# Chunk 0 loaded as three transfers of 1 MB, its attention run tensor by tensor

## The chip, the cores and the metric

The kernel runs on one core of a Trainium2 chip. The metric is the device time of one execution in microseconds (us); lower is better.

The core has a TensorE (PE in the profile, with its weight loads as PEld), a VectorE (DVE), a ScalarE (ACT), a GpSimd (POOL) and a SyncE (SP). Each has its own stream of instructions and runs it in order. The streams wait for each other through semaphores. Transfers between HBM and on-chip memory are issued from the streams of SP, ACT and POOL, and appear in the profile as the queues q1 (issued on SP), q10 (ACT) and q0 (POOL).

## The reference

The input is q, k and v of shape (4 batches, 8 heads, 768 steps, 64) in float32 and two weights. A linear attention with a decay per head feeds a two-layer network with GELU:

```
for t in 0..767:
    state = gamma_h * state + outer(k_t, v_t)        # per batch and head, 64 x 64
    y_t   = scale * q_t @ state
x   = y as (3072 tokens, 512)
out = gelu_tanh(x @ w_in) @ w_out                    # 512 -> 2048 -> 512
```

## The kernel before

**Tiling.** The 768 steps are cut into six chunks of 128 (`C`). For a chunk `c` and a batch `b` the attention has these steps, each a helper:

- `prep1(eng, nm, c, b)` casts one of q, k, v of one batch (128 steps x 8 heads x 64) to float16 on the engine named, with the decay multiplied in (line 162) or as a plain copy (`copy_on`, lines 149 and 151).
- `mm_T` (line 192) transposes q and k of a batch on TensorE, eight instructions, and `ev_T` copies them to on-chip memory as `qkT`.
- `mm_A` (line 217) makes the 128 x 128 products of k and q within a chunk, and `ev_A` (line 230) multiplies them by `mask` on VectorE into `a_sb`, two buffers per half.
- `mm_yc` (line 241) adds the part of the earlier state and does nothing for chunk 0. `mm_yi` (line 254) makes the part within the chunk, and `ev_Y` copies the result to `xT`.
- `mm_s` (line 278) makes this chunk's addition to the state, and `ev_S` folds it into `st`. The state is first needed by Y of chunk 1.

The first layer of the network is called M1 here: `moe1` (512 tokens, one block of 128 features) and `moe1_two` (two blocks of features, a range of tokens `t0` to `t1`), both through `moe1_mm` (line 363), with a GELU on ScalarE (line 379). `t01` is the tokens of batches 0 and 1, `t2` and `t3` those of batches 2 and 3. The second layer of chunk 0 is `moe2` (line 397). For chunks 1 to 5 the two layers are made from sums of quarter blocks (lines 434, 507 and 622), which take most of the span.

**Order.** There is no planner. The kernel is written under a manual schedule: each engine runs its instructions in the order in which the Python calls stand. Chunk 0 is written out by hand, and the change lies there. `spin(n)` puts n matmuls of zeros on TensorE (line 126).

**Loads.** `load1(eng, nm, c, b)` (line 89) moves one tensor of one batch and chunk, 256 KB. `load(nm, c, eng)` (line 95) moves a tensor of all four batches, 1 MB, on SP unless told otherwise; it is used from chunk 2 on. Chunk 0 comes as twelve `load1`, dealt out over SP and ACT in the order in which the batches need them:

```
    nc.sync.dma_start(out=cst[:, :OT + 128], in_=cst_h.ap())
    load1(nc.scalar, "q", 0, 0)
    load1(nc.sync, "k", 0, 0)
    load1(nc.scalar, "v", 0, 0)
    ...
```

`cst` holds the decays and the triangle from which VectorE makes `mask` (line 137, eight instructions), and `iden` is the identity for the transposes. `load_w_in(i)` (line 344) and `load_w_out(i)` (line 353) each move one quarter of a weight from float32 to float16, 1 MB read and 512 KB written, on POOL. POOL reaches `load_w_in(0)` behind its scaling of k of batch 1, and the other three behind that of batch 2. `hold` (line 102) is a one-element copy on POOL that keeps chunk 1's loads back until a weight has landed.

**Chunk 0.** The batches go one after the other: prep, transposes, A, Y and S of batch 0, then of batch 1, and so on, with spins between them. Y of batches 0 and 1 stands before M1, and batches 2 and 3 are woven into M1's first groups. M1's groups 4 and 5 are made as two ranges of 256 tokens, groups 6 to 15 with all 512.

Of the kernel before, what the change touches and what calls it, by code (L numbers as in the profile page):

```python
# [9 lines left out]
F16 = mybir.dt.float16  # L10
# [6 lines left out]
def kernel(  # L17
# [9 lines left out]
    nc = tc.nc  # L27
    B, H, S, Dh = q.shape
# [59 lines left out]
    def load1(eng, nm, c, b):  # L88
        eng.dma_start(
            out=ld_tile(nm, c, b),  # L90
            in_=srcs[nm][b, :, c * C:(c + 1) * C, :].rearrange("h p d -> p h d"),
        )
# [8 lines left out]

        nc.gpsimd.tensor_copy(out=ld_tile(nm, c, b)[0:1, 0, 0:1], in_=until)

    nc.sync.dma_start(out=cst[:, :OT + 128], in_=cst_h.ap())
    load1(nc.scalar, "q", 0, 0)
    load1(nc.sync, "k", 0, 0)
    load1(nc.scalar, "v", 0, 0)
    nc.sync.dma_start(out=iden, in_=iden_h.ap())
    load1(nc.sync, "q", 0, 1)
    load1(nc.scalar, "k", 0, 1)  # L110
    load1(nc.sync, "v", 0, 1)
    load1(nc.sync, "k", 0, 2)
    load1(nc.sync, "q", 0, 3)
    load1(nc.sync, "v", 0, 3)


    zero = const.tile([128, 512], F16, name="zero")
# [5 lines left out]
    def spin(n):  # L123
        ps = bank("h", shape=(128, 512), name="spin_ps")
        for _ in range(n):
            nc.tensor.matmul(
                out=ps, lhsT=zero[:, 0:128], rhs=zero, start=True, stop=True
            )
# [16 lines left out]
    h16 = {}  # L145
# [7 lines left out]
    def prep1(eng, nm, c, b):  # L153
        t = pre.tile(
            [128, H, Dh], F16, tag=f"{nm}16", bufs=B, name=f"{nm}16"
        )
        src = ld_tile(nm, c, b)
        if (nm == "v") == (c < 2):
            copy_on(eng, t, src)
        else:  # L160
            col = OQ if nm == "q" else OK
            eng.tensor_tensor(  # L162
                out=t,
                in0=src,
                in1=cst[:, col:col + H].unsqueeze(2).broadcast_to([128, H, Dh]),
                op=ALU.mult,
            )
        h16[nm, c, b] = t

    def pair(t, hp):  # L170
        return t[:, 2 * hp:2 * hp + 2]
# [16 lines left out]
    def mm_T(c, b):  # L188
        ps = bank("att", F16, (128, 2, NHP, 128), "qkT_ps")
        for i, nm in enumerate("qk"):  # L190
            for hp in range(NHP):
                nc.tensor.transpose(  # L192
                    out=ps[:, i, hp], in_=pair(h16[nm, c, b], hp), identity=iden
                )
        pss["T", c, b] = ps
# [6 lines left out]
    def ev_T(c, b, eng=nc.vector):  # L202
        copy_on(eng, qkT_of(c, b), pss.pop(("T", c, b)))

    def dma_T(nm, c, *bs):
        for b in bs:
            nc.sync.dma_start_transpose(
                out=qkT_of(c, b)[:, "qk".index(nm)],
                in_=h16[nm, c, b].rearrange("p h d -> p (h d)"),
            )  # L210

    def mm_A(c, b):
        t = qkT[c, b]
        ps = [bank("att", name=f"a_ps{j}") for j in range(2)]
        for hp in range(NHP):
            for j in range(2):
                nc.tensor.matmul(  # L217
                    out=ps[j][:, hp],
                    lhsT=t[j * 64:(j + 1) * 64, 1, hp],
                    rhs=t[j * 64:(j + 1) * 64, 0, hp],  # L220
                    start=True,
                    stop=True,
                )
        pss["A", c, b] = ps

    def ev_A(c, b):
        ps = pss.pop(("A", c, b))
        for j in range(2):
            s = att.tile([128, NHP, 128], F16, tag=f"a{j}", bufs=2, name=f"a_sb{j}")
            nc.vector.tensor_tensor(out=s, in0=ps[j], in1=mask[:, j], op=ALU.mult)  # L230
            a_sb[c, b, j] = s

    def mm_yc(c, b, tag):
        y_ps = pss["Y", c, b] = bank(tag, name="y_ps")
        if c == 0:
            return

        for hp in range(NHP):
            for j in range(2):
                sl = slice(j * 64, (j + 1) * 64)  # L240
                nc.tensor.matmul(  # L241
                    out=y_ps[sl, hp],
                    lhsT=st[sl, b, hp],
                    rhs=qkT[c, b][sl, 0, hp],
                    start=(hp == 0),
                    stop=False,
                    skip_group_check=True,
                )

    def mm_yi(c, b):  # L250
        y_ps = pss["Y", c, b]
        for hp in range(NHP):
            for j in range(2):
                nc.tensor.matmul(  # L254
                    out=y_ps[j * 64:(j + 1) * 64, hp],
                    lhsT=h16["v", c, b][:, 2 * hp + j],
                    rhs=a_sb[c, b, j][:, hp],
                    start=(c == 0),
                    stop=True,
                    skip_group_check=True,  # L260
                )

    def ev_Y(c, b, eng=nc.vector):
        if c not in xT:
            xT[c] = xp.tile([128, NHP, B * C], F16, tag="x", bufs=2, name="xT")
        x, ps = xT[c][:, :, b * C:(b + 1) * C], pss.pop(("Y", c, b))
        if c < 2:
            copy_on(eng, x, ps)
        else:
            nc.vector.tensor_tensor(out=x, in0=ps, in1=dec, op=ALU.mult)  # L270

    def mm_s(c, bs, tag="att"):
        if c + 1 >= NCk:
            return
        s_ps = pss["S", c, bs] = bank(tag, shape=(128, len(bs), NHP, 64), name="s_ps")
        for i, b in enumerate(bs):
            for h in range(H):
                nc.tensor.matmul(  # L278
                    out=s_ps[h % 2 * 64:(h % 2 + 1) * 64, i, h // 2],
                    lhsT=h16["k", c, b][:, h],  # L280
                    rhs=h16["v", c, b][:, h],
                    start=True,
                    stop=True,
                )

    def ev_S(c, bs, eng=nc.vector):
        if c + 1 >= NCk:
            return
        s_ps = pss.pop(("S", c, bs))
        t = st[:, bs[0]:bs[-1] + 1]  # L290
        if c == 0:
            copy_on(eng, t, s_ps)
            return
        for hp in range(NHP):
            nc.vector.scalar_tensor_tensor(
                out=t[:, :, hp],
                in0=t[:, :, hp],
                scalar=cst[:, OG + hp:OG + hp + 1],
                in1=s_ps[:, :, hp],
                op0=ALU.mult,  # L300
                op1=ALU.add,
            )
# [40 lines left out]
    def load_w_in(i):  # L343
        nc.gpsimd.dma_start(
            out=w_in_sb[i],
            in_=moe_w_in.rearrange("(kc p) n -> p kc n", p=128)[
                :, :, w_in_at[i] * 128:(w_in_at[i] + w_in_n[i]) * 128
            ],
        )
# [36 lines left out]
    def moe1_two(c, fp, t0, t1):  # L386

        h_ps = bank("h", shape=(128, 2, B * C // 2), name="h_ps")
        for r in range(2):
            moe1_mm(c, 2 * fp + r, h_ps[:, r, 0:t1 - t0], t0, t1)  # L390
        gelu(g_tile(c, 2 * fp)[:, :, t0:t1], h_ps[:, :, 0:t1 - t0])
# [269 lines left out]
    half = 2 * C  # L661


    load1(AC, "q", 0, 2)
    load1(AC, "v", 0, 2)
    spin(14)
    prep1(VE, "q", 0, 0)
    prep1(PO, "k", 0, 0)
    prep1(AC, "v", 0, 0)
    mm_T(0, 0)  # L670
    ev_T(0, 0, AC)
    load1(AC, "k", 0, 3)
    prep1(VE, "q", 0, 1)
    prep1(PO, "k", 0, 1)
    spin(3)
    mm_A(0, 0)
    ev_A(0, 0)
    mm_T(0, 1)
    ev_T(0, 1, AC)
    prep1(AC, "v", 0, 1)  # L680
    spin(2)
    mm_yc(0, 0, "o")
    mm_yi(0, 0)
    mm_s(0, (0,), "o")
    ev_Y(0, 0, AC)
    prep1(VE, "q", 0, 2)

    load_w_in(0)
    prep1(PO, "k", 0, 2)
    for i in range(1, 4):  # L690
        load_w_in(i)
    prep1(PO, "k", 0, 3)
    prep1(PO, "q", 0, 3)
    for i in range(NO):
        load_w_out(i)
    mm_A(0, 1)
    ev_A(0, 1)
    spin(3)
    mm_T(0, 2)
    ev_T(0, 2, AC)  # L700
    spin(2)
    mm_yc(0, 1, "o")
    mm_yi(0, 1)
    mm_s(0, (1,), "o")
    ev_Y(0, 1, AC)
    prep1(AC, "v", 0, 2)
    spin(2)
    mm_A(0, 2)
    ev_A(0, 2)
    ev_S(0, (0,), AC)  # L710
    prep1(AC, "v", 0, 3)
    ev_S(0, (1,), AC)
    spin(6)
    mm_T(0, 3)
    ev_T(0, 3)


    t01, t2, t3 = (0, half), (half, half + C), (half + C, 2 * half)
    moe1_two(0, 0, *t01)
    mm_A(0, 3)  # L720
    ev_A(0, 3)
    mm_yc(0, 2, "o")
    mm_yi(0, 2)
    mm_s(0, (2,))
    ev_Y(0, 2, AC)
    moe1_two(0, 1, *t01)
    ev_S(0, (2,))
    moe1_two(0, 0, *t2)
    moe1_two(0, 1, *t2)
    mm_yc(0, 3, "o")  # L730
    mm_yi(0, 3)
    mm_s(0, (3,))
    ev_Y(0, 3)
    ev_S(0, (3,))
    moe1_two(0, 2, *t01)
    for fp in range(2):
        moe1_two(0, fp, *t3)
    moe1_two(0, 2, half, 2 * half)

    hold("q", 1, 0, w_out_sb[2][0:1, 0, 0:1])  # L740
    for fc in range(6, NF):
# [210 lines left out]
```

## Time and profile before

| | us |
|---|---|
| median of 3 runs (lowest to highest) | 207.66 (206.92 to 209.23) |
| the profiled execution, its own time | 207.1 |
| its span, first to last instruction | 205.0 |
| PE busy | 195.2 (95%) |
| DVE, ACT, POOL busy | 128.3, 120.6, 110.8 |
| start of M1 of chunk 0 | 18.45 |
| start of the second layer of chunk 0 | 34.81 |

The span is counted from the first to the last instruction of one execution; its own time has 2.1 us more around it. The busy share of an engine is a mean over stages with different limits. The chain of waits, followed back from the last instruction, is 82% TensorE's own work and 8% waiting for transfers. In a line of the timeline the columns are start, length, engine, line of the kernel, operation, output and input, and the count. Lines that read `q1 hardware_dynamic: a, b, c%` give the packets, the megabytes and the share of the sixteen DMA engines of one queue in a stretch of time. The list of DMA issues gives the KB of one transfer and the microseconds from issue to landing; for the transfers of 1 MB the size in this list is misread as 0.2 KB.

### The profile page before, as it was taken

To read this page: it belongs to the slowest core of one execution; us is meant where nothing else is said; L and a number is where in the kernel's file an instruction comes from. 1 tells how busy PE (TensorE), PEld (TensorE's weight loads), DVE (VectorE), ACT (ScalarE), POOL (GpSimd) and SP (SyncE) were. 2 spreads that over 40 slices of the span, in tenths; PEclk is the share of its full clock that TensorE was granted. 3 is DMA by queue.
4 is the path that set the end of the run, shared out by engine and by line. 5 is a ranking of instruction groups with operands and counts; after the bars stand their busy time and mean duration, and the time that the engine had idled before them with its cause. 6 is when DMAs were issued, how large, how long until landed. Compare 5 with 4: busy or idle time off the path is not lost.

```text
span 205.0 us, 5216 instructions
## 1 busy us (share of the span) xinstructions
PE 195.2 (95%) x2120; PEld 151.6 (74%) x2120; DVE 128.3 (63%) x259; ACT 120.6 (59%) x229; POOL 110.8 (54%) x112
## 2 busy tenths in 40 slices
PE   7868999999999989999999999999999999999993
PEld 2445744445778867788887888888888888888882
DVE  3335796429876689989853888836697723445421
ACT  2481566143478457853978585878555587675411
POOL 0597001223103993926399948399955797599000
PEclk9999999999999999999999999999999999999999
DMA  7999999989899993459958869953100220002204
GB/s 160 288 261 206 206 207 221 287 203 297 238 328 220 240 313 84 100 118 298 253 135 202 229 146 307 95 156 128 26 3 0 101 107 0 5 0 106 102 26 179
DMA packets 60759, 33.73 MB, mean 165 GB/s; under 512 B 40960, under 2 KB 57728, under 8 KB 60736
## 3 DMA queue, kind: packets, MB, share of 16 engines
q1 hardware_dynamic: 42624, 22.66, 43.9%
q0 software_dynamic: 4304, 4.46, 12.7%
q10 hardware_dynamic: 13808, 6.29, 11.9%
q8 instruction: 16, 0.26, 0.5%
q14 instruction: 7, 0.06, 0.1%
HBM read 27.63 MB, written 6.29 MB: 165 GB/s over the span
## 4 chain that ended last, share of the span: by engine, by line
PE 82%; DMA 8%; DVE 3%; ACT 3%; issue 1%; ACTq 1%; POOL 0%; DVEq 0%
PE o_ps L507 28%; PE h_ps L622 23%; PE h_ps L363 13%; PE o_ps L397 7%; DMA w_in<-in_moe_w_in_dram 5%; PE y_ps L254 3%; PE a_ps L217 3%; DMA k<-in_k_dram 3%; PE y_ps L241 3%; ACT g L379 1%; DVE xT L270 1%; PE qkT_ps L192 1%; PE s_ps L278 1%; ACTq L95 1%; DVE t_x L434 1%
## 5 line engine op out<-in xcount | busy, mean ns | idle before, releaser
L434 POOL TENSOR_TENSOR s_g<-g 128x512 f16<-128x512 f16 x34 | 38.7, 1151 | 11.6 <-ACT g L379 11.6
L379 ACT ACTIVATE g<-h_ps 128x512 f16<-128x512 f32 (+1 forms) x50 | 28.8, 581 | 22.9 <-PE h_ps L363 17.7
L230 DVE TENSOR_TENSOR a_sb<-a_ps,mask 128x512 f16<-128x512 f32 x48 | 30.2, 684 | 8.8 <-PE a_ps L217 8.4
L507 PE MATMUL o_ps<-t_w,s_g 128*128 128x256 f16 x240 | 34.2, 273 | 0.0
L507 PEld LDWEIGHTS <-s_g 128*128 128x128 f16 x320 | 31.3, 98 | 3.6
L363 PE MATMUL h_ps<-xT,w_in 128*128 128x256 f16 (+2 forms) x232 | 30.4, 284 | 1.2 <-DMA w_in<-in_moe_w_in_dram 0.7
L622 PE MATMUL h_ps<-t_x,s_w 128*128 128x256 f16 x192 | 28.9, 273 | 0.3 <-DVE h_p L434 0.3
L622 PEld LDWEIGHTS <-s_w 128*128 128x128 f16 x256 | 24.4, 98 | 4.7 <-issue 1.2
L363 PEld LDWEIGHTS <-w_in 128*128 128x128 f16 x232 | 20.6, 98 | 8.5 <-issue 0.9
L507 PEld LDWEIGHTS <-g 128*128 128x128 f16 x240 | 23.4, 98 | 2.8
L507 PE MATMUL o_ps<-w_out,g 128*128 128x256 f16 x160 | 22.9, 273 | 0.0
L162 POOL TENSOR_TENSOR v<-v,cst 128x512 f16<-128x512 f32 x16 | 16.2, 1038 | 11.2 <-DMA v<-in_v_dram 11.2
L434 POOL TENSOR_TENSOR s_g<-s_g,g 128x512 f16<-128x512 f16 x17 | 19.6, 1155 | 4.6 <-PE o_ps L507 3.4
L639 ACT COPY h_u<-h_ps 128x512 f32<-128x512 f32 x16 | 9.4, 586 | 21.3 <-PE h_ps L622 21.3
L434 DVE TENSOR_TENSOR h_q<-h_ps,h_q 128x512 f32<-128x512 f32 x16 | 11.1, 692 | 16.3 <-PE h_ps L622 10.4
L622 PEld LDWEIGHTS <-w_in 128*128 128x128 f16 x192 | 18.3, 98 | 3.4 <-issue 0.7
L434 POOL TENSOR_TENSOR s_g<-g,s_g 128x512 f16<-128x512 f16 x17 | 19.5, 1156 | 0.5
L434 DVE TENSOR_TENSOR h_p<-h_ps,h_p 128x512 f32<-128x512 f32 x16 | 11.0, 690 | 13.7 <-ACT h_p L639 9.4
L622 PE MATMUL h_ps<-xT,w_in 128*128 128x256 f16 x128 | 19.2, 272 | 0.3 <-ACT g L379 0.3
L162 POOL TENSOR_TENSOR k<-k,cst 128x512 f16<-128x512 f32 x8 | 8.8, 1094 | 17.7 <-DMA k<-in_k_dram 16.3
L434 DVE TENSOR_TENSOR o_sb<-o_ps,o_sb 128x512 f32<-128x512 f32 (+1 forms) x18 | 10.8, 597 | 7.6 <-PE o_ps L507 7.3
L397 PE MATMUL o_ps<-w_out,g 128*128 128x512 f16 x64 | 14.8, 379 | 0.0
(71 smaller groups left out, 301.0 us busy)
## 6 DMA issues: line engine op xcount, KB each, us to landing
out_dram<-o_sb SPq DMA_DIRECT2D x8, 512.0 KB, 2.7
w_in<-in_moe_w_in_dram POOLq DMA_DIRECT2D x4, 512.0 KB, 9.9
w_out<-in_moe_w_out_dram POOLq DMA_DIRECT2D x4, 512.0 KB, 14.6
k<-in_k_dram SPq DMA_DIRECT2D x6, 256.0 KB, 4.9
v<-in_v_dram ACTq DMA_DIRECT2D x6, 256.0 KB, 5.6
q<-in_q_dram SPq DMA_DIRECT2D x6, 256.0 KB, 5.2
out_dram<-o_sb SPq DMA_DIRECT2D x4, 256.0 KB, 4.4
q<-in_q_dram ACTq DMA_DIRECT2D x2, 256.0 KB, 4.9
```

Of the source, the lines that this page charges most:

```text
L162: eng.tensor_tensor(out=t, in0=src, in1=cst[:, col:col + H].unsqueeze(2).broadcast_to([128, H, Dh]), op=ALU.mult,)
L217: nc.tensor.matmul(out=ps[j][:, hp], lhsT=t[j * 64:(j + 1) * 64, 1, hp], rhs=t[j * 64:(j + 1) * 64, 0, hp], start=True, stop=True,)
L230: nc.vector.tensor_tensor(out=s, in0=ps[j], in1=mask[:, j], op=ALU.mult)
L241: nc.tensor.matmul(out=y_ps[sl, hp], lhsT=st[sl, b, hp], rhs=qkT[c, b][sl, 0, hp], start=(hp == 0), stop=False, skip_group_check=True,)
L254: nc.tensor.matmul(out=y_ps[j * 64:(j + 1) * 64, hp], lhsT=h16["v", c, b][:, 2 * hp + j], rhs=a_sb[c, b, j][:, hp], start=(c == 0), stop=True,
L363: nc.tensor.matmul(out=out, lhsT=w_in_sb[wi][:, kc, wr * 128:(wr + 1) * 128], rhs=xT[c][:, kc, t0:t1], start=(kc == 0), stop=(kc == NHP - ...
L379: nc.scalar.activation(out=out, in_=in_, func=AF.Gelu_apprx_tanh, scale=1.0)
L397: nc.tensor.matmul(out=ps[:, n0:n1], lhsT=g_sb[c, fc // 8][:, fc % 8, b * C:(b + 1) * C], rhs=w_out_sb[fc // (NF // NO)][:, fc % (NF // NO ...
L434: eng.tensor_tensor(out=out, in0=in0, in1=in1, op=op)
L507: nc.tensor.matmul(out=po, lhsT=lhs(c, lk, fp, a), rhs=rhs(rk, fp), start=(new and fp == 0 and (last or a == 0)), stop=(fp == NP - 1), ski ...
L622: nc.tensor.matmul(out=p[:, f], lhsT=w, rhs=x, start=(new and f == 0 and kk == 0), stop=(kk == 1), skip_group_check=True,)
L639: nc.scalar.copy(out=snap[nm], in_=p)
```

## The change

Chunk 0's k, q and v are issued on SP as three transfers of 1 MB, in that order. `cst` and `iden` move from SP to ACT's queue. The twelve `load1`, three of which stood among ACT's work, are gone.

The attention of chunk 0 then runs tensor by tensor. All four k are scaled on VectorE and transposed, with a new helper `one_T` that transposes one tensor of one batch and evacuates it on ACT into its half of `qkT`; then all four q; then v is cast, batches 0 and 3 on ACT, 1 and 2 on POOL. All four A stand before M1, as do Y of batches 0 and 1. Y of batches 2 and 3 stands between M1's first groups. S of all batches is made two batches at a time behind those groups, evacuated on VectorE. M1's groups 4 and 5 are made with all 512 tokens.

w_in's four quarters are triggered on POOL together, behind a one-element copy that reads the first scaled k. w_out's four follow POOL's two casts of v. The numbers of spins change to 13, 6, 2 and 2.

```diff
-    nc.sync.dma_start(out=cst[:, :OT + 128], in_=cst_h.ap())
-    load1(nc.scalar, "q", 0, 0)
-    load1(nc.sync, "k", 0, 0)
-    load1(nc.scalar, "v", 0, 0)
-    nc.sync.dma_start(out=iden, in_=iden_h.ap())
-    load1(nc.sync, "q", 0, 1)
...
+    nc.scalar.dma_start(out=cst[:, :OT + 128], in_=cst_h.ap())
+    for nm in "kqv":
+        load(nm, 0)
+    nc.scalar.dma_start(out=iden, in_=iden_h.ap())
...
+    def one_T(nm, c, b, eng):
+        i = "qk".index(nm)
+        ps = bank("att", F16, (128, NHP, 128), "qkT_ps")
+        for hp in range(NHP):
+            nc.tensor.transpose(out=ps[:, hp], in_=pair(h16[nm, c, b], hp), identity=iden)
+        copy_on(eng, qkT_of(c, b)[:, i], ps)
...
-    load1(AC, "q", 0, 2)
-    load1(AC, "v", 0, 2)
-    spin(14)
-    prep1(VE, "q", 0, 0)
-    prep1(PO, "k", 0, 0)
-    prep1(AC, "v", 0, 0)
-    mm_T(0, 0)
-    ev_T(0, 0, AC)
...
+    spin(13)
+    for b in range(B):
+        prep1(VE, "k", 0, b)
+        one_T("k", 0, b, AC)
+        if b == 0:
+            nc.gpsimd.tensor_copy(out=misc[0:1, 2:3], in_=h16["k", 0, 0][0:1, 0, 0:1])
+            for i in range(4):
+                load_w_in(i)
+    spin(6)
+    for b in range(B):
+        prep1(VE, "q", 0, b)
+        one_T("q", 0, b, AC)
+        if b == 2:
+            mm_A(0, 0)
     ev_A(0, 0)
...
+    for b in (0, 3):
+        prep1(AC, "v", 0, b)
+    for b in (1, 2):
+        prep1(PO, "v", 0, b)
     for i in range(NO):
         load_w_out(i)
     mm_A(0, 1)
     ev_A(0, 1)
-    spin(3)
-    mm_T(0, 2)
-    ev_T(0, 2, AC)
+    spin(2)
+    mm_yc(0, 0, "o")
+    mm_yi(0, 0)
+    ev_Y(0, 0, AC)
+    mm_A(0, 2)
+    ev_A(0, 2)
     spin(2)
     mm_yc(0, 1, "o")
     mm_yi(0, 1)
-    mm_s(0, (1,), "o")
     ev_Y(0, 1, AC)
...
+    mm_A(0, 3)
+    ev_A(0, 3)
     t01, t2, t3 = (0, half), (half, half + C), (half + C, 2 * half)
     moe1_two(0, 0, *t01)
-    mm_A(0, 3)
-    ev_A(0, 3)
     mm_yc(0, 2, "o")
     mm_yi(0, 2)
-    mm_s(0, (2,))
     ev_Y(0, 2, AC)
     moe1_two(0, 1, *t01)
...
-    moe1_two(0, 2, *t01)
-    for fp in range(2):
-        moe1_two(0, fp, *t3)
-    moe1_two(0, 2, half, 2 * half)
+    for t in (t2, t3):
+        for fp in range(2):
+            moe1_two(0, fp, *t)
+    for bs in ((0, 1), (2, 3)):
+        mm_s(0, bs)
+        ev_S(0, bs)
+    for fc in range(4, 6):
+        moe1(0, fc)
```

More of the change, by code (lines that the diff above doesn't have):

```diff
@@ L102, in hold @@
         nc.gpsimd.tensor_copy(out=ld_tile(nm, c, b)[0:1, 0, 0:1], in_=until)
-    nc.sync.dma_start(out=cst[:, :OT + 128], in_=cst_h.ap())
-    load1(nc.scalar, "q", 0, 0)
-    load1(nc.sync, "k", 0, 0)
-    load1(nc.scalar, "v", 0, 0)
-    nc.sync.dma_start(out=iden, in_=iden_h.ap())
-    load1(nc.sync, "q", 0, 1)
[L110 to L114, printed above, removed]
+    nc.scalar.dma_start(out=cst[:, :OT + 128], in_=cst_h.ap())
+    for nm in "kqv":
+        load(nm, 0)
+    nc.scalar.dma_start(out=iden, in_=iden_h.ap())
     zero = const.tile([128, 512], F16, name="zero")
@@ L661 @@
     half = 2 * C
-    load1(AC, "q", 0, 2)
-    load1(AC, "v", 0, 2)
-    spin(14)
-    prep1(VE, "q", 0, 0)
-    prep1(PO, "k", 0, 0)
-    prep1(AC, "v", 0, 0)
-    mm_T(0, 0)
-    ev_T(0, 0, AC)
-    load1(AC, "k", 0, 3)
-    prep1(VE, "q", 0, 1)
-    prep1(PO, "k", 0, 1)
-    spin(3)
-    mm_A(0, 0)
-    ev_A(0, 0)
[L678 to L693, printed above, removed]
+    spin(13)
[12 more added lines that the diff above has]
+            mm_A(0, 0)
+    ev_A(0, 0)
+    for b in (0, 3):
+        prep1(AC, "v", 0, b)
+    for b in (1, 2):
+        prep1(PO, "v", 0, b)
     for i in range(NO):
@@ L697 @@
     ev_A(0, 1)
-    spin(3)
-    mm_T(0, 2)
-    ev_T(0, 2, AC)
+    spin(2)
[4 more added lines that the diff above has]
+    ev_A(0, 2)
     spin(2)
@@ L703 @@
     mm_yi(0, 1)
-    mm_s(0, (1,), "o")
     ev_Y(0, 1, AC)
[L706 to L715, printed above, removed]
+    mm_A(0, 3)
+    ev_A(0, 3)
     t01, t2, t3 = (0, half), (half, half + C), (half + C, 2 * half)
     moe1_two(0, 0, *t01)
-    mm_A(0, 3)
-    ev_A(0, 3)
     mm_yc(0, 2, "o")
     mm_yi(0, 2)
-    mm_s(0, (2,))
     ev_Y(0, 2, AC)
     moe1_two(0, 1, *t01)
-    ev_S(0, (2,))
-    moe1_two(0, 0, *t2)
-    moe1_two(0, 1, *t2)
     mm_yc(0, 3, "o")
     mm_yi(0, 3)
-    mm_s(0, (3,))
     ev_Y(0, 3)
-    ev_S(0, (3,))
-    moe1_two(0, 2, *t01)
-    for fp in range(2):
-        moe1_two(0, fp, *t3)
-    moe1_two(0, 2, half, 2 * half)
+    for t in (t2, t3):
[6 more added lines that the diff above has]
+        moe1(0, fc)
     hold("q", 1, 0, w_out_sb[2][0:1, 0, 0:1])
```

## The prediction

> **What bounds the kernel now.** I read the page's engine shares first (PE 95% of 205.0 us), then the chain of waits, to see where the rest lies, then the timeline and the DMA queues of the first 35 us, where every edit lies. The chain of the first 35 us:
>
> ```profile
> 1.85 5.94 DMA k<-in_k_dram
> 7.79 0.07 issue
> 7.86 0.99 POOL k L162
> 8.85 9.55 DMA w_in<-in_moe_w_in_dram
> 18.41 0.04 issue
> 18.45 1.05 PE h_ps L363 x8
> ...
> 24.70 10.11 PE h_ps L363 x56
> ```
>
> Columns are start, length, what. Until 18.45 the core waits for data: k of batch 1, its scaling on POOL, then w_in's first quarter. From 18.45 on TensorE runs almost without a pause, as the busy times by stage say (length, then PE, PEld, DVE, ACT, POOL):
>
> ```profile
> 18.45:34.81 16.36, 15.88 (x145) 10.02 (x146) 12.82 (x34) 9.67 (x18) 1.15 (x3) 1.00 1.24 206
> 34.81:60.00 25.19, 25.19 (x251) 14.68 (x250) 15.14 (x33) 9.86 (x19) 5.05 (x5) 1.00 1.01 267
> ```
>
> So the price of the change is the shift of M1's start (18.45) plus the change in M1's stretch (16.36). In the next stage PE has no idle time, and later gaps sum to under 2 us; a shift reaches the end nearly whole.
>
> Why does w_in land 9.55 us after its trigger? The queues from 10 to 12, from 13 to 14 and from 16 to 17 us (packets, MB, share):
>
> ```profile
> q10 hardware_dynamic: 1206, 0.30, 67.4%
> q1 hardware_dynamic: 1078, 0.27, 60.1%
> ...
> q1 hardware_dynamic: 668, 0.17, 76.0%
> q0 software_dynamic: 90, 0.09, 54.7%
> ...
> q0 software_dynamic: 198, 0.19, 115.4%
> q8 instruction: 1, 0.02, 5.8%
> ```
>
> w_in's queue q0, triggered at 8.85, moves nothing until 13.3: it starts as chunk 0's loads (q1, q10), all issued by 9.52, run dry. Its 512 packets then take 2.5 us at 205 packets/us. The trace's landing records show 15 of its 16 parts done by 16.66 and the last at 18.41: that DMA engine also carried the 16 KB instruction fetch (q8) at 16.36. So 1.75 us of the wait is one late engine.
>
> **The change part by part.** *Loads.* Twelve 256 KB loads on two queues become three of 1 MB on SP, 0.73 us on. The trace has the same three back to back, at 88.64 on SP, with landing times in the list of issues:
>
> ```profile
> 88.64 0.70 SPq L95 DMA_DIRECT2D q<-in_q_dram  x1
> 89.79 3.22 SPq L95 DMA_DIRECT2D k<-in_k_dram  x1
> 93.47 3.19 SPq L95 DMA_DIRECT2D v<-in_v_dram  x1
> ...
> q<-in_q_dram SPq DMA_DIRECT2D x1, 0.2 KB, 6.0
> k<-in_k_dram SPq DMA_DIRECT2D x1, 0.2 KB, 8.6
> v<-in_v_dram SPq DMA_DIRECT2D x1, 0.2 KB, 9.3
> ```
>
> Counted from the first issue they land at 6.0, 1.15 + 8.6 = 9.75 and 4.83 + 9.3 = 14.1 us. For the changed kernel: k 6.75, q 10.5, v 14.8. Bounds: at the 342 GB/s that this queue holds between the dips of that stretch (96 to 97 us), 3.15 MB take 9.2 us from the first packet at 2.0, v landing at 11.8; with w_in sharing, 19.0 (below). I take 14.8, the row of the same form. The old loads end at 14.4, so nothing is won on bytes.
>
> *k and the trigger.* DVE scales k (0.69 each, L162's row on DVE) instead of POOL (1.04). The first is done at 7.5, POOL's one-element copy costs 0.27 (L102's row), w_in is triggered near 7.9, 0.9 us sooner, its four issues taking 0.93 + 3 x 0.77 us. Queued behind POOL's copy are only w_in, the two v copies and w_out. SP's issue of v ends near 0.73 + 8.02 = 8.75, as in the row above, so v is accepted about when w_in0 is. By what w_in0 did before, it then waits for the dry queue: v's last packets near 14.1, plus 2.5, lands at 16.7. PE's instruction fetch came after about 222 issued TensorE instructions; in the new order that lies behind M1's first groups, so it should not fall on w_in0.
>
> *q on DVE.* 10.5 + 4 x 0.69 = 13.3; then the masks of A, 1.29 per batch: A0 14.6, A1 15.9, A2 17.2, A3 18.5. ACT's eight half evacuations (bound 0.59 to 1.01) lie beside these. The transposes and four A (0.4 each) lie in PE's idle time.
>
> *v.* 14.8 + 0.65 (cast on ACT) = 15.5; Y0 0.4, A2 0.4, two spins 0.43, while POOL copies v1. POOL has no row for this copy: bounds 0.69 (DVE's copy) and 1.17 (POOL's slowest scaling); I take 1.05, done 15.9, hidden behind those PE steps, at most 0.3 on the path if they vanish. Y1 then runs 16.75 to 17.15 and ACT evacuates it in 0.59: M1 starts at 17.8. This chain, v plus 3.0, now ends last, before w_in's 16.7 is asked for. It replaces the 18.45.
>
> *M1's stretch.* Out of 16.36 go A3 (0.33) and two half-width pairs for feature groups 4 and 5, 4 x 0.495 = 1.98 against 2 x 0.865 = 1.73; S of batches 0 and 1 come in, 0.12 to 0.25 each. I take 16.36 - 0.33 - 0.25 + 0.3 = 16.1. GELU pauses (two of 0.24 before) may stay. M1 ends at 33.9 instead of 34.81: **0.9 us gained**.
>
> *What costs nothing.* S's state copies on DVE are due by Y of chunk 1 (48.3). w_out is triggered after POOL's v copies, near 17 to 20 instead of 16 to 19; its queue is full with w_in until 25, and its first quarter (issued 16.0, landed 12.0 us later) is due at 33.9. If w_in ended early this cover goes, at most 1 us, still 4 us ahead of need. Chunk 1's loads hang on w_out and the last GELUs and keep over 1 us of slack (k of batch 1 scaled by 44.4, transposed at 47).
>
> The Trainium skill, "DMA: Bandwidth & Descriptors" (Queues, rings and completion order), speaks against this: each DMA engine goes round robin between its queue rows at packet granularity. By that rule w_in, in the rings from about 9, would halve v's pace, and the sum would be that of rival 1; the row of w_in0 here shows no such sharing, the row at 33 us does.
>
> **Rivals.** *1, sharing, slower.* From 28 to 33 us a load arrives on q10 while q0 is busy:
>
> ```profile
> q0 software_dynamic: 994, 0.99, 119.1%
> q10 hardware_dynamic: 72, 0.02, 2.8%
> ```
>
> It begins 2 us late and then gets one packet for each of q0's (151 of q0 and 155 of q10 from 33 to 34). If w_in's packets enter at 9.3 (8.0 plus 1.15, the delay of POOL's store at 52.85), about 1.2 MB of q and v are left (the loads at 88 us had moved 1.95 of 3.15 MB 8.6 us after their first issue): 73 packets of 1 KB per engine, each paired with one of w_in, 47 ns (16 / 342 GB/s) + 78 ns (16 / 205 per us) = 125 ns, so 9.1 us. v lands at 19.0, M1 starts at 22.0 and ends at 38.1: +3.3, 210.4 us. It decides once w_in enters before about 11.5. For it: the single ring, with dips between its transfers. Against: w_in0's 4.4 us wait in the same situation.
>
> *2, a slow TensorE clock.* The first 14 spins take 0.43 us each where later ones take 0.22, until about 7 us, though the page's clock row says 9 throughout. The change drops from 30 spins to 23, and between 11 and 17.8 us PE is busy some 5 us of 7, before nearly all. If M1 starts at half pace, the 5.6 us that the spins took cost 2.8: +1.9, 209.0. The gap of 1.6 us at 13.15 did no harm before.
>
> The skill's "TensorE: Matmul & The Clock Gate" (Part 1: The HAM clock gate) names idle windows of about 3.4 us as what throttles; no gap so long is expected here, and none is in the trace, so by the rule this rival would fall.
>
> *3, the stream at full rate.* v at 11.8 and q at 8.7 leave DVE's chain: q + 4 x 0.69 + 2 x 1.29 + 1.9 = 15.9; M1 ends at 32.0: -2.8, 204.3. For: the 342 GB/s stretches; against: the 1 MB loads at 88 and at 119 us both dip between transfers.
>
> *4, no effect.* A fetch delays w_in0 again: M1 at 18.45, -0.3, 206.8.
>
> **How the numbers follow.** The profiled execution took 207.1 us around its span of 205.0; the median of the three runs is 207.66 (206.92 to 209.23). The sum is 207.1 - 0.9 = 206.2 there; the runs to be compared lie around the median, so 206.8, and I state 206.7. My forecast has 0.37 (own range 205.6 to 207.6), rival 1 0.26, rival 2 0.12, rival 3 0.21, rival 4 0.04. The range 204.0 to 211.0 reaches rival 3 and rival 1 on the median. One per cent (2.1 us) is about what a measurement of this kernel can tell from no change. Faster by more: rival 3 and a sixth of the forecast, 0.27. Slower by more: rival 1 nearly whole, half of rival 2 and a little of the forecast, 0.34. Within: 0.39.
>
> **What would show it.** Right: k, q, v landing near 6.75, 10.5, 14.8; no q0 packets before 13; the first M1 group released by ACT's Y evacuation, not by w_in, at 17.8; M1 ending near 33.9; then no new gap. Wrong: q0 and q1 packets side by side from 9 to 18 us with v near 19 (rival 1); M1 groups of 512 at well over 0.865 (rival 2); v under 13 (rival 3). A PE gap after 34 us that before did not have would overturn the claim that the shift passes whole.

## The result, and the profile after

The changed kernel is slower: 213.54 us (median of 4 runs, 213.33 to 214.8) against 207.29 for the kernel before, a ratio of 1.030 (95% interval 1.023 to 1.037). Forecast was 206.7, with a range of 204.0 to 211.0. Medians here and below are over all executions, while ratios count only the fast ones, leaving out an execution that is more than 1.5% above the fastest of its kernel. The profiled execution is the one of 214.8, with a span of 213.0 and a mean granted clock of 0.959 against 0.972 to 0.974 in the others, so some 1.3 us of what its trace shows are its own.

The chain of waits of the changed kernel, up to the second layer:

```profile
6.45 14.85 DMA v<-in_v_dram
21.30 0.02 issue
21.32 0.63 ACT v L142
...
21.99 0.64 PE y_ps L254 x8
22.63 0.54 PE a_ps L217 x8
23.17 0.96 PE spin_ps L119 x2
24.14 0.59 PE y_ps L254 x5
...
25.38 1.86 PE h_ps L363 x8
...
32.03 10.47 PE h_ps L363 x48
42.50 0.65 PE o_ps L397 x3
```

M1 starts at 25.38 instead of 18.45, and what holds it is the chain that the prediction named: v, its cast, Y, A, two spins, Y, the evacuation. But v lands at 21.30 and not at 14.8, and the chain behind it takes 4.08 us and not 3.0. The second layer starts at 42.33 instead of 34.65 (both are its first matmul in the timeline; the chains show 42.50 and 34.81). From there to the last matmul it is 167.1 us, against 166.8 before: the shift passes to the end whole. So 6.9 us of the 8.0 by which this span is longer come ahead of M1, 0.75 in M1's stretch (16.95 instead of 16.20), 0.3 behind it.

The queues of the changed kernel from 11 to 12 and from 12 to 20 us (packets, MB, share), where the kernel before had w_in waiting until 13.3:

```profile
q0 software_dynamic: 114, 0.12, 84.8%
q1 hardware_dynamic: 13, 0.01, 7.1%
...
q0 software_dynamic: 980, 0.97, 71.7%
q1 hardware_dynamic: 968, 0.99, 44.5%
```

From 12 to 20 us w_in (q0) and v (q1) go packet for packet. v needs 1024 packets of 1 KB; at 121 of them per us they end near 20.5. This is rival 1.

TensorE's row at the end of that wait, and the granted clock by stage (the number ahead of the last two):

```profile
21.99 0.64 PE L254 MATMUL y_ps<-a_sb,v 128*64 128x128 f16 x8 [5.38 <-ACT v L142]
```

```profile
18.00:21.00 3.00, 0.00 (x0) 0.00 (x0) 0.00 (x0) 0.00 (x0) 0.00 (x0) 0.50 1.19 240
24.00:27.00 3.00, 2.86 (x25) 1.83 (x24) 1.78 (x3) 0.58 (x1) 1.43 (x2) 0.50 1.21 192
29.00:42.00 13.00, 12.97 (x119) 7.18 (x120) 10.67 (x28) 8.43 (x16) 0.81 (x2) 1.00 0.91 163
```

TensorE stands still for 5.38 us for v. Its clock is at half from 17.9 to 28.2, so that Y takes 0.64 where full pace gives 0.41, and M1's first eight matmuls 1.86 instead of 1.05. This is rival 2, on top of rival 1.

Why did w_in share this time? The two issues in the changed kernel, on SP and on POOL:

```profile
6.45 3.39 SPq L95 DMA_DIRECT2D v<-in_v_dram  x1
```

```profile
8.86 0.93 POOL L344 DMA_DIRECT2D w_in<-in_moe_w_in_dram  x1
```

v's issue ended at 9.84, that of w_in's first quarter at 9.79. In the kernel before the issue of the last load ended at 9.52 and that of w_in's first quarter at 9.78:

```profile
7.76 1.76 SPq L89 DMA_DIRECT2D v<-in_v_dram  x1
```

```profile
8.85 0.93 POOL L344 DMA_DIRECT2D w_in<-in_moe_w_in_dram  x1
```

The theory that the experiments test is that this order decides: what a queue finished issuing earlier is served first, and w_in shares with what was finished later. Its rival is that w_in slips in because SP's single queue runs dry for a moment between q and v (11 to 12 us above).

### The profile page after: what moved, and what is told of

Same layout as the page of the kernel before. It is cut to its first block, busy times and chain, and to the rows that moved or that the text cites. A ratio compares the mean times of both kernels' runs of the same rounds, so it can differ in the third digit from the quotient of the medians.

```text
span 213.0 us, 5172 instructions
## 1 busy us (share of the span) xinstructions
PE 198.0 (93%) x2103; PEld 152.1 (71%) x2103; DVE 131.2 (62%) x263; ACT 121.0 (57%) x230; POOL 107.4 (50%) x110
## 4 chain that ended last, share of the span: by engine, by line
PE 79%; DMA 9%; DVE 4%; ACT 3%; SPq 3%; issue 1%; DVEq 0%; ACTq 0%
PE o_ps L507 25%; PE h_ps L622 21%; PE h_ps L363 14%; DMA v<-in_v_dram 7%; PE o_ps L397 7%; PE y_ps L254 4%; PE a_ps L217 3%; PE y_ps L241 3%; SPq L95 3%; DMA qkT<-k 2%; PE qkT_ps L185 1%; PE s_ps L278 1%; DVE xT L270 1%; ACT g L379 1%; ACT q L142 1%
## 5 line engine op out<-in xcount | busy, mean ns | idle before, releaser
L363 PE MATMUL h_ps<-xT,w_in 128*128 128x256 f16 (+2 forms) x224 | 31.4, 294 | 0.2
L363 PEld LDWEIGHTS <-w_in 128*128 128x128 f16 x224 | 20.1, 99 | 8.5 <-issue 0.4
L622 PEld LDWEIGHTS <-w_in 128*128 128x128 f16 x192 | 18.3, 98 | 3.7 <-issue 0.8
L397 PE MATMUL o_ps<-w_out,g 128*128 128x512 f16 x64 | 14.8, 379 | 0.0
L254 PE MATMUL y_ps<-a_sb,v 128*64 128x128 f16 x192 | 9.1, 234 | 5.4 <-ACT v L142 5.4
## 6 DMA issues: line engine op xcount, KB each, us to landing
w_in<-in_moe_w_in_dram POOLq DMA_DIRECT2D x4, 512.0 KB, 11.8
```

The lines of the kernel that those rows point to most:

```text
L254: nc.tensor.matmul(out=y_ps[j * 64:(j + 1) * 64, hp], lhsT=h16["v", c, b][:, 2 * hp + j], rhs=a_sb[c, b, j][:, hp], start=(c == 0), stop=True,
L363: nc.tensor.matmul(out=out, lhsT=w_in_sb[wi][:, kc, wr * 128:(wr + 1) * 128], rhs=xT[c][:, kc, t0:t1], start=(kc == 0), stop=(kc == NHP - ...
L397: nc.tensor.matmul(out=ps[:, n0:n1], lhsT=g_sb[c, fc // 8][:, fc % 8, b * C:(b + 1) * C], rhs=w_out_sb[fc // (NF // NO)][:, fc % (NF // NO ...
L622: nc.tensor.matmul(out=p[:, f], lhsT=w, rhs=x, start=(new and f == 0 and kk == 0), stop=(kk == 1), skip_group_check=True,)
```

## The experiments

All times are medians against the kernel before on the same chip, which took 206.3 to 206.5 there. Each edit is against the changed kernel unless said.

### w_in triggered behind v

```diff
-            nc.gpsimd.tensor_copy(out=misc[0:1, 2:3], in_=h16["k", 0, 0][0:1, 0, 0:1])
+            nc.gpsimd.tensor_copy(out=misc[0:1, 2:3], in_=ld_tile("v", 0, 0)[0:1, 0, 0:1])
```

> The changed kernel, but the copy that holds w_in's triggers back reads v instead of the first scaled k, so w_in is triggered when v has landed. Theory 1 (w_in's packets pair with v's one for one and that is the main loss): v lands near 15.1 instead of 21.3 (q's 11.4 plus 3.7), w_in is triggered near 15.5, its first quarter lands near 19.4, M1 starts near 19.5 and the time is 207.5 to 209.5. Theory 2 (the slow TensorE clock is the main loss): the spins are as few as before, so most of the loss stays, 211 or more. Theory 3 (three 1 MB transfers on one queue are slow by themselves): v still lands near 20, M1 starts after 25, 214 or more.

210.79 us, ratio 1.019 (1.013 to 1.025). v landed at 14.97: alone, SP's three transfers give what the row at 88 us had promised (14.8). w_in then came too late, M1 at 20.63, and TensorE waited a further 2.46 us at 66.9 for k of chunk 2, which the expected 207.5 to 209.5 had not counted. The sharing is the cause of v's delay; the three transfers are not.

### q on ACT's queue

```diff
-    for nm in "kqv":
-        load(nm, 0)
+    load("k", 0)
     nc.scalar.dma_start(out=iden, in_=iden_h.ap())
+    load("q", 0, nc.scalar)
+    load("v", 0)
```

> The changed kernel, but q's 1 MB is issued on ACT's queue, behind iden; k and v stay on SP and w_in's trigger stays at the first scaled k. Theory 1, with the rule that what was accepted by the queues before w_in goes first: SP accepts v sooner, its issue ends before w_in's first at 8.9, w_in waits as it did in the kernel before, v lands near 15, w_in's first quarter near 17, M1 starts near 18, and the time is 206 to 208. If w_in pairs with whatever is left however early it was accepted: v stays at 19 or later and the time at 211 or more. Theory 3 expects v near 15 too, with the gain from two queues, but w_in would still begin near 11.

206.29 us, ratio 0.999 (0.996 to 1.001). With one transfer less ahead of it, v's issue ended at 5.54, and w_in (issue ended 9.50) moved nothing until 12.2. v landed at 13.44, w_in's first quarter at 15.88. What set M1's 18.44 was something else:

```profile
9.85 0.56 PE qkT_ps L210 x4
10.41 2.56 PE spin_ps L120 x6
...
18.44 1.03 PE h_ps L364 x8
```

These are rows of this variant's chain. The six spins between k and q, at half clock, stand in front of q's transposes.

### The kernel before, with w_in triggered early

```diff
     prep1(PO, "k", 0, 0)
+    for i in range(4):
+        load_w_in(i)
...
-    load_w_in(0)
     prep1(PO, "k", 0, 2)
-    for i in range(1, 4):
-        load_w_in(i)
```

> The kernel before, with all four of w_in's triggers moved up on POOL, right behind the scaling of k of batch 0, near 6.6 instead of 8.9 and 11.7. SP and ACT accept the last loads only by 8.6 and 9.5. Rule of acceptance: the loads accepted after about 7.5 (batch 3's k and v, perhaps its q) pair with w_in's packets, move at about a fifth of their pace, and land 5 us or more later; Y and A of batches 2 and 3 slip behind M1's start. k of batch 1 also waits for POOL's four issues, 3 us. w_in's first quarter lands 1 to 2 us sooner, but the time is 208 to 212. If earlier w_in simply helps: below 206.

213.86 us, ratio 1.035 (1.030 to 1.040). The twelve loads on two queues never run dry, and w_in shares all the same with those three that were issued after it. From 13 to 14 us:

```profile
q0 software_dynamic: 137, 0.14, 81.1%
q1 hardware_dynamic: 135, 0.03, 26.0%
q10 hardware_dynamic: 135, 0.03, 15.2%
```

The last v landed at 26.39. An early trigger alone, without any of the change's loads, makes the kernel before as slow as the changed one. Not all of that need be sharing: POOL's scaling of k of batch 1 now stands behind the four issues and starts at 9.92 instead of 7.86.

### Twelve loads, tensor by tensor, on both queues

```diff
-    for nm in "kqv":
-        load(nm, 0)
     nc.scalar.dma_start(out=iden, in_=iden_h.ap())
+    for nm in "kqv":
+        for b in range(B):
+            load1((nc.sync, nc.scalar)[b % 2], nm, 0, b)
```

> The changed kernel's order of work with the loads as twelve of 256 KB, all k, then all q, then all v, batches 0 and 2 on SP, 1 and 3 on ACT, behind cst and iden. Theory 1 with the rule of acceptance: the last loads are accepted near 9.5, w_in's first quarter near 9, so at most the last two v pair with it: v complete between 14.5 and 17, M1 at 18 to 20, 207 to 209. Theory 3 (the 1 MB form is the cause): v at 14.5 and w_in's first quarter near 17, M1 near 18, 206 to 207. If w_in pairs with everything left at 10 us whatever the form: packets of 256 B paired with w_in's make v land after 22 and the time 214 or more.

218.59 us, ratio 1.056 (1.049 to 1.063). Small loads let the first k land sooner, so w_in was triggered at 5.10, when only seven of the twelve loads had been issued; the last v was issued by 14.64 and landed at 26.56. A trigger that hangs on data gets earlier with the data, and more of the loads fall behind it. The expected 207 to 209 took the trigger to stay where it was.

### One copy more, three copies more

The first experiment moved w_in by 6 us, the second moved a queue. The tie can be broken by much less, with the one-element copy on POOL made several times (here four):

```diff
-            nc.gpsimd.tensor_copy(out=misc[0:1, 2:3], in_=h16["k", 0, 0][0:1, 0, 0:1])
+            for i in range(4):
+                nc.gpsimd.tensor_copy(out=misc[0:1, 2 + i:3 + i], in_=h16["k", 0, 0][0:1, 0, 0:1])
```

Two copies:

> The changed kernel with two one-element copies on POOL instead of one ahead of w_in's triggers. In the changed kernel the issue of w_in's first quarter ended at 9.79 (8.86 + 0.93) and that of v at 9.84 (6.45 + 3.39), a tie to 0.05 us. Theory A, the queue whose issue ends first goes first: the copy (taken as 0.27) moves w_in's end to about 10.1, behind v, so v is not shared, lands near 15, w_in's first quarter waits for it and lands near 17, M1 starts at 18.0 to 18.6 and the second layer near 34: 206.5 to 211, the upper part if chunk 2's k then comes late as it did with w_in triggered at 12.38. Theory B, w_in enters because SP's queue is empty for a moment between q and v (10.5 to 11 us): 0.3 us changes nothing, its first packets come near 10.8, v lands at 21, 213 to 214.

Four copies:

> The same with four copies: the issue of w_in's first quarter ends 0.8 us or more later than the changed kernel's 9.79, at 10.6 or later, and 0.8 behind v's 9.84. Theory A (the queue whose issue ends first goes first): v lands near 15, w_in's first quarter near 17, M1 at 18.0 to 18.6, the second layer near 34, 206.5 to 211. Theory B (the moment between q and v lets it in): v's first packets come near 11.0 and w_in's near 11.3, after the moment, but they may still pair from there: v 20 to 21, 212 to 214.

Two copies: 208.54 us over all 12 runs, 208.09 over the nine that the ratio of 1.005 (1.001 to 1.009) counts. Four copies: 207.44 over all 12, 207.15 over the eight that the ratio of 1.002 (0.999 to 1.005) counts. The runs go from 206.5 to 211.9 with both, and what made the longest of them was not traced. The queues of the version with two copies from 10 to 11, 12 to 13 and 14 to 15 us:

```profile
q1 hardware_dynamic: 177, 0.16, 83.1%
...
q1 hardware_dynamic: 334, 0.34, 105.5%
...
q0 software_dynamic: 121, 0.12, 72.6%
q1 hardware_dynamic: 120, 0.12, 44.2%
```

SP's queue has its thin stretch between q and v here too (177 packets in a microsecond, 334 two microseconds later), and w_in does not slip in: it enters at 13.1, when most of v is through, and shares the rest; v lands at 16.73 and the second layer starts at 36.59. With four copies w_in enters at 14.3, when v is nearly through (it lands at 15.28), M1 starts at 18.28 and the second layer at 33.98. The moment between q and v is not the cause; how far the issue of one ends ahead of the other's is.

In one table: when the issues ended, and how many MB of chunk 0's loads (`cst` and `iden` included; 3.25 in all) had moved when w_in's eighth packet came, summed from the packets in the traces. The rows with spins and with one quarter early are of experiments that follow.

| kernel | loads' issue ended | w_in's first ended | MB moved |
|---|---|---|---|
| before | last at 9.52 | 9.78 | 3.2 |
| changed | v at 9.84 | 9.79 | 2.2 (k and q) |
| 24 spins | v at 9.40 | 9.48 | 2.2 (k and q) |
| 30 spins | v at 9.98 | 9.78 | 2.2 (k and q) |
| one quarter early | v at 9.69 | 9.56 | 2.2 (k and q) |
| two copies | v at 9.54 | 9.97 | 2.9 |
| four copies | v at 9.82 | 10.92 | 3.2 |
| q on ACT | v at 5.54 | 9.50 | 3.2 |
| before, early w_in | nine of 12 by 7.70 | 7.70 | 2.45 (nine are 2.46) |
| twelve loads | seven of 12 by 6.03 | 6.03 | 1.9 (seven are 1.9) |

A lead of 0.08 us was not enough for v, 0.43 saved most of it, 1.10 nearly all. So it is not the bare order of the ends that decides; a lead is needed, and how much of one lies somewhere between 0.08 and 1.10 us in these runs.

### What the clock cost: 24 and 30 spins

```diff
     ev_A(0, 1)
-    spin(2)
+    spin(30)
     mm_yc(0, 0, "o")
```

24:

> The changed kernel with 24 spins instead of 2 ahead of Y of batch 0, which fill the 5.4 us in which TensorE waits for v. Theory 1: the DMA times do not change (v at 21.3); only the cold part goes: Y, A and spins from v to M1 in 3.0 instead of 4.1 us and M1's first groups at 0.99 instead of 1.86 and 1.17, about 2 us in all: 211 to 212. Theory 2: the clock is the main loss, 208 or less. If the clock has no part in it: 213.5.

30:

> The changed kernel with 30 spins ahead of Y of batch 0. With 24 they ended at 20.4, v's cast came at 22.4, and the granted clock fell to half between 22.5 and 26. With 30 they end near 21.8, so the pause is under 1 us. Clock theory: the clock stays up from 15 on, v to M1 takes 3.1 instead of 4.0 us, M1's first groups take 0.99 each, and the time is 211 to 212, some 2 us under the changed kernel, which is the whole price of the clock; the rest, over 4 us, stays with v. If the clock has no part: 213 as with 24.

213.12 (ratio 1.032, 1.026 to 1.038) and 213.44 us (1.033, 1.029 to 1.036): no gain, where 211 to 212 was expected of both. With 24 the spins ended at 20.44 and v came at 21.76, and the clock still fell, from 22.5 to 26.0. With 30 it stayed at 1.00 from 14 us on:

```profile
6.45 16.50 DMA v<-in_v_dram
...
22.97 0.63 ACT v L142
...
25.95 1.03 PE h_ps L363 x8
```

From v to M1 it is now 3.0 us instead of 4.08, and M1's stretch is 15.70 instead of 16.95: the half clock had cost 2.3 us. That price holds for the profiled execution of the changed kernel, whose mean clock was 0.959; the means of 0.972 to 0.974 in its other executions come to some 6 us less at half clock (an estimate from the means and spans), so they may have paid less, and none of them was traced. Against the gain, v landed at 22.95, 1.65 later than in the changed kernel's profile. Its last part alone accounts for 0.9 of that: the other fifteen were in by 22.04, and an instruction fetch (16 KB on queue q8) ran at 20.15. That the spins brought the fetch there is likely, since it came at 19.50 with 24 spins and at 25.03 with 2; that it held v's last part back is inferred from the times. The rest was lost at the start: w_in's issue had ended 0.20 ahead of v's here and 0.05 in the changed kernel, and from 11 to 13 us v's queue moved 7 packets here and 124 there.

### What a later or a split w_in costs further on

```diff
...
+        if b == 0:
+            nc.gpsimd.tensor_copy(out=misc[0:1, 2:3], in_=h16["q", 0, 0][0:1, 0, 0:1])
+            for i in range(4):
+                load_w_in(i)
```

Here the trigger stands behind the first scaled q instead of k.

> The changed kernel with one thing moved: w_in's triggers stand behind the first scaled q instead of the first scaled k, so near 12.0 instead of 8.9. All three loads stay on SP. Theory 1 with the rule of acceptance (SP's issue of v ends near 9.8): v is accepted before w_in, so w_in waits until v is through; v lands near 15, w_in's first quarter near 17.5, M1 starts near 18.3 and the time is 206.5 to 208.5. If what helped in the kernel with q on ACT was the second queue and not the order of acceptance: w_in's packets enter near 13.5 and pair with v's rest, v lands near 17, M1 at 20.5, 209 or more.

211.09 us, ratio 1.023 (1.017 to 1.028). Up to the second layer it went as wanted: w_in triggered at 12.38, v in at 15.07, M1 at 18.36, the second layer at 34.07. What the expected 206.5 to 208.5 had not counted is at 63.2, where TensorE waits 2.7 us for k of chunk 2. Its chain, and the queues from 56 to 60 and from 60 to 63 us:

```profile
49.90 15.21 DMA k<-in_k_dram
...
65.19 0.62 ACT k L142
```

```profile
q10 hardware_dynamic: 992, 1.01, 88.9%
q1 hardware_dynamic: 69, 0.07, 5.6%
...
q1 hardware_dynamic: 910, 0.93, 103.4%
q10 hardware_dynamic: 53, 0.05, 6.3%
```

It is the same order again, now between SP and ACT: k's issue on SP lasted from 49.90 to 56.23, v's on ACT from 54.46 to 55.29, and v's whole megabyte went first. In the kernel before k's issue had ended at 54.20 and v's began at 54.96, and from 55 to 59 us 1013 packets of k passed against 23 of v.

```diff
-            for i in range(4):
-                load_w_in(i)
+            load_w_in(0)
...
+    for i in range(1, 4):
+        load_w_in(i)
```

> The changed kernel, but only w_in's first quarter is triggered behind the first scaled k; the other three follow POOL's two casts of v. Theory 1 as a dose: v then pairs with 512 packets of w_in instead of some 1,050, so it lands 2.5 us sooner, near 18.5 instead of 21.3, M1 starts near 22.5 (the later quarters are due only from group 4 on and land from about 23), and the time is 210 to 211.5. If only the fact that w_in came first counts, and not how much of it: v at 21, 213 or more. If sharing has no part: no change, 213.5.

One quarter early, three behind POOL's casts of v: 215.79 us, ratio 1.047 (1.043 to 1.050), the expectation missed by 4 us. M1 started at 20.51, sooner than in the changed kernel, but w_out landed near 43 instead of 37.4, and chunk 1's loads, which hang on it, began at 40.55 (39.37 in the changed kernel, 33.98 in the kernel before), though the second layer now started at 36.22 and not at 42.33. TensorE then waited 0.67 and 0.90 at 46 for q and k of chunk 1, and 2.71 at 67 for k of chunk 2, whose issue ended at 60.48, behind v's at 59.35, as in the experiment ahead of this one; from 71.3 to 74.7 its clock was at half. The stream of weights has a due time of its own.

### A version that beats both

Both are made from the version with q on ACT. First, two of the six spins kept:

```diff
-    spin(6)
+    spin(2)
```

> The kernel with q's load on ACT, and 2 spins instead of 6 ahead of q's transposes. In that kernel q had landed at 10.6 and its first scaling was done at 11.3, but the spins, at half clock, held TensorE until 12.8, so VectorE's masks of A waited from 13.1 to 14.5. Theory 1, now with the chain on VectorE as the bound: A0's mask starts near 13.2, M1 starts near 17.1 instead of 18.4 (w_in's first quarter is there at 15.9), and the time is 204.5 to 205.5. If the clock theory holds instead: the spins were needed, TensorE runs M1's first groups at half clock and the gain is lost, 206 to 208. If neither sets the start: 206.3 as it was.

207.60 us over all 12 runs (204.89 to 208.55), 206.35 over the eight that the ratio of 1.001 (0.998 to 1.005) counts. With fewer spins M1 starts 1.15 us sooner (17.29), but no gain in time is shown. The mean granted clocks differ, from 0.988 in the profiled 205.94 to between 0.972 and 0.975 in all seven runs over 207; that the missing spins cost the clock there is likely and was not traced. Then the spins spread out:

```diff
-    spin(13)
+    spin(16)
     for b in range(B):
         prep1(VE, "k", 0, b)
         one_T("k", 0, b, AC)
+        spin(1)
...
-    spin(6)
     for b in range(B):
         prep1(VE, "q", 0, b)
         one_T("q", 0, b, AC)
+        if b < 2:
+            spin(1)
```

> The kernel with q's load on ACT, with the spins laid out anew: 16 at the start instead of 13, one behind each k's transposes, none in a block ahead of q's, one behind the transposes of q of batches 0 and 1. TensorE is meant to be busy from 1.2 to 11.4 without holding up q's transposes. If the chain on VectorE sets M1's start and the clock stays up: M1 near 17.4, 205.0 to 205.8, without the spread up to 208.5 of the kernel with 2 spins. If the clock falls all the same: a spread of 205 to 208. If neither counts: 206.3.

205.44 us (12 runs, 205.03 to 206.80), ratio 0.995 (0.993 to 0.997). Its chain and its clock from 5 us on:

```profile
1.79 8.78 DMA q<-in_q_dram
...
10.59 0.70 DVE q L156
...
17.20 1.03 PE h_ps L364 x8
...
22.60 10.46 PE h_ps L364 x48
33.07 3.02 PE o_ps L398 x14
```

```profile
18.00:33.00 15.00, 14.97 (x140) 8.43 (x138) 11.28 (x30) 9.77 (x18) 0.57 (x2) 1.00 1.24 205
5.00:17.00 12.00, 9.21 (x98) 4.52 (x96) 8.70 (x15) 6.75 (x12) 7.28 (x11) 1.00 1.17 292
```

With v (13.34) and w_in (15.79) out of the way, q and VectorE's masks set M1, 1.25 us sooner than before. The gain in time is half a per cent: with its loads issued in time and its spins spread out, the order of work in the change is worth about 1 us here.

## Why the prediction was wrong

**The step that failed** is the sentence "SP's issue of v ends near 0.73 + 8.02 = 8.75, as in the row above, so v is accepted about when w_in0 is. By what w_in0 did before, it then waits for the dry queue". Its own numbers held the warning: w_in triggered at 7.9 with an issue of 0.93 is complete at 8.83, 0.08 behind v's 8.75. I called a tie a case and took the side on which the kernel before had been, where the lead was 0.26. The trace gave 9.79 against 9.84, and the row with 24 spins shows that a lead of 0.08 would not have been enough either. The question to ask of the old trace was not whether w_in had shared but what it had waited for.

**What the runs showed in its place.** With the two issues ending this close, w_in moves from 10.6 on, v is shared packet for packet, lands at 21.30 instead of 14.8 and puts M1 at 25.38 instead of 17.8.

**What of the forecast was right.** Unshared, v lands at 14.97, 15.07 or 15.28 (14.8 forecast). M1's stretch at full clock is 15.70 (16.1 forecast). The chain from v to M1 is 3.0 at full clock, as summed. That the shift would pass whole held: 167.1 us behind the second layer's start against 166.8. Where the tie is broken by four copies, the second layer starts at 33.98 against the forecast 33.9, and the time is 207.15 to 207.44 against 206.7. Part of this agreement is luck: M1 starts 0.48 later than the sum had it (18.28), and its stretch is 0.4 shorter. Nor is it v's chain that ends last there, though v's cast is done only 0.1 us sooner; it is k's, through six spins and q's transposes, which the sum had put into TensorE's idle time:

```profile
10.34 2.21 PE spin_ps L119 x6
12.55 1.43 PE qkT_ps L209 x12
...
18.28 1.03 PE h_ps L363 x8
```

**Sizes that were off.** k landed at 7.56, not 6.75, and POOL's one-element copy cost 0.52 up to the trigger (0.27 taken), so the trigger came at 8.86, not 7.9. q's issue took 3.88 where the row at 88 had 3.22. POOL's cast of v took 0.61, below the lower bound of 0.69 and well below the 1.05 taken, at no effect, since it is hidden.

**Rival 1** (26%) is what happened: queues side by side, v late. It said v at 19.0, M1 at 22.0. v came 2.3 us later: the sharing began near 11.5, not at 9.3 (8.0 plus 1.15 is 9.15, a small slip in the sum), with v untouched, so that its 64 packets per DMA engine all found a partner, at 132 ns a pair (16 engines, 121 pairs per us) where 125 was worked out. Its condition ("once w_in enters before about 11.5") was met, and its time was the upper end of the range. What carried the result beyond 211.0 is this later v, and rival 2 on top of it; the run with 30 spins, with the clock up and v later still, took 213.44.

**Rival 2** (12%) was costed as a case of its own, with 0.43 us spins from the start of the trace. The rivals are not exclusive: sharing makes TensorE wait for v, and the wait takes the clock. Its price, 2.3 us in the profiled execution by the run with 30 spins, is near the 1.9 plus 0.9 that separate it from the forecast. The text said "no gap so long is expected here"; the gap was 5.38 us. **Rival 3** (v at 11.8) came nowhere near: alone on the queue, the three transfers still took until 14.97 and 15.07. **Rival 4** did not come: no fetch fell on w_in's first quarter.

**Rules and rows.** The Trainium skill, "DMA: Bandwidth & Descriptors" (Queues, rings and completion order) has each DMA engine take turns between its queue rows, packet by packet. The 980 and 968 packets from 12 to 20 us agree with it, as do the three nearly equal counts of the early trigger; that w_in's eighth packet comes 2.7 to 3.7 us after its issue behind loads issued clearly earlier, and 0.8 to 1.3 us after it otherwise, is measured here, and the rule by itself would not give it. I weighed rule against row as if one had to be wrong; both hold, and the lead of one issue over the other says when. The skill's "TensorE: Matmul & The Clock Gate" (Part 1: The HAM clock gate) spoke of idle windows of about 3.4 us. The gap of 5.38 us is longer than that, but the clock fell at 17.93, 1.3 us after the last spin ahead of the gap (16.61), so no such window had passed yet: the measurement does not agree with the rule as it stands.

## What to carry to other kernels

When a large transfer is moved or triggered earlier, write down for every queue when its issue ends, not when it begins, and compare: in these runs what was complete clearly first went first, and what came at about the same time or after was shared, so that a margin of a few tenths of a microsecond was worth five. A tie in such a sum is two cases with a price each, not a detail; and a trigger that hangs on data moves when the data does. Price a new wait of TensorE with what it does to the clock behind it.

## What the hardware showed that I had not expected

- **Order of issue across queues.** Loads on SP's and ACT's queues are not dealt out evenly either: in the run with w_in behind q, 992 packets of ACT's v passed against 69 of SP's k, whose issue ended 0.94 us later, and then 910 of k's. Once w_in has entered, though, it keeps its turn through its later quarters, which were issued up to 12.01, after v. Why it waits on entry and not afterwards is open.
- **A long issue.** In the changed kernel the issue of a 1 MB load took 0.86 us on an empty queue and 3.4 to 3.9 behind another; behind k and q, v's ended 9 us after the first issue began. Moving q to another queue brought v's end forward by 4.3 us (9.84 to 5.54).
- **The clock needs less than 3.4 us without work to fall.** Its changes in the traces stand 3.4 us, or a multiple of that, apart. In the run with two copies TensorE was busy 1.67 of the 3.60 us up to 18.6 (longest gap 1.93), in that with four 1.85 of the 3.40 up to 10.6, and both had half clock next; the kernel before was busy 2.04 of the 3.40 from 13.4 (gap 1.60) and kept it. The share of busy time does not settle it either: the kernel before with early w_in was busy 1.84, 1.60 and 1.87 of the three times 3.41 us up to 25.6, stood still for 3.36 us in one piece up to 23.74, and kept full clock. What decides is open.
